# Turning the last third of one batch's tokens by DMA instead of on TensorE, under a new order of the whole program

## The chip, the cores and the metric

The kernel runs on one core of a Trainium2 chip. A core has several engines that run side by side, each with its own list of instructions: TensorE (PE: matmuls, with a weight load ahead of each), VectorE (DVE), ScalarE (ACT), GpSimd (POOL) and SyncE (SP, which here only issues DMAs). They wait for each other through semaphores. The metric is the device time of one execution in microseconds (us); the time of a kernel is the median of several executions.

## The reference

Sliding-window attention with four sink tokens for 4 batches, 8 heads, 768 tokens and 64 columns a head, and then a feed-forward layer on its output:

```python
keep = (pos[None, :] < 4) | ((rel >= 0) & (rel < 128))      # rel = query - key
scores = np.where(keep, q @ k.T / 8, -1e9)
a = softmax(scores)                                          # per row
x = (a @ v), heads side by side                              # 3072 tokens x 512
g = np.maximum(x @ w_in, 0) ** 2                             # w_in  512 x 2048
out = g @ w_out                                              # w_out 2048 x 512
```

Inputs and outputs are fp32; the kernel computes in bf16 with fp32 sums.

## The kernel before, in words

A batch b has 768 tokens: six tiles of 128 tokens (0 to 5), or three pairs of tiles s = 0, 1, 2. Its eight heads are four pairs m = 0 to 3. The work of a batch has these stages:

- **Loads.** For batch 1, q and k come with a cast to bf16 as `qn` (tokens on partitions), by DMAs that GpSimd issues (`load_cast`, L355); v likewise. Batches 2 and 3 do the same in `load_natural` (L383).
- **Turning q and k.** Scores need q and k with the head's columns on partitions (`qkT`). For batches 0 and 1 TensorE turns blocks of 128 x 128 by a matmul with the identity into PSUM (`pt`, L500), and VectorE or ScalarE copies PSUM to `qkT` (L191, L189). For batches 2 and 3 (the list `NATURAL`), SyncE issues one transposing DMA for each tile of q and of k (L454), straight from `qn` to `qkT`.
- **Scores** (L607), **exp** (ScalarE, L628), **mask** (two triangles on GpSimd, L215, or one product on VectorE, L640), **sink scores** and **sink_values** (the parts of the four sinks), **values** (L676, `po`), and **norm**: VectorE's reciprocal (L692) and product into `xn_sb` (L693).
- **Turning the attention output** (`xn_sb` to `xT`). For batches 0 and 1 two "bridge" operations for a pair of tiles turn it on TensorE (L725, into `px`), and two copies take it to `xT`. For batches 2 and 3 `turn_x` (L707) does it by a transposing DMA for each tile.
- **Layer 1** (`x @ w_in`; L757 for batches 0 and 1, seven products of a Strassen kind, L887, with sums on VectorE, L928 and L955, for batches 2 and 3), relu on ScalarE or VectorE (L768, L770), the square (L909, L911), and **layer 2** (L976, L1086), copies out of PSUM (`taken`, L1105) and the stores.

Batch 1's work is done in two groups of tokens: g = 0 is tiles 0 to 3, g = 1 is tiles 4 and 5 (the last third, s = 2).

The order is written out by hand or by a search, not found while the program runs. The kernel's functions only register operations with a `Plan`; `ORDER`, a text of operation numbers (a letter behind a number gives the engine where there is a choice), says in which order they are issued, and that is each engine's own program order. An operation that waits holds up everything behind it on its engine; so a DMA on SyncE that waits for its data holds up the DMAs behind it. Semaphore waits come from the data's dependencies, and from the reuse of buffers: PSUM pools att and den (two each), and SBUF pools (expm 8, r 3, sg 4, osb 2 and others).

`touch` (L196) keeps the list of instructions that use parts of one PSUM tile, and declares two of them independent when they are on different banks and either one of them is TensorE's, or both are marked `alone` and sit on different engines. `use` (L1067) calls it for layer 2's PSUM tile, `taken` copies one of its quarters out.

`NATURAL, TURNED, BIASED, FAST = (2, 3), (), 1, (2, 3)` (L1183) is the switch: `TURNED` lists the pairs of tiles of batch 1 whose attention output is turned by DMA, and it is empty. `BIASED` and `FAST` name where a mask is added by a matmul and where the seven products are used.

## Time and profile before

| what | value |
|---|---|
| median of 3 executions | 212.43 us (212.35 to 212.47) |
| the profiled execution's own time | 212.79 us |
| its span, from the first to the last instruction | 211.1 us |
| mean granted TensorE clock | 0.998 |
| busy TensorE, VectorE, ScalarE, GpSimd | 202.7, 171.3, 124.0, 98.0 us |

The profile is one execution. A line of a timeline or of the chain gives start, length, engine, line of the kernel, operation, output <- inputs and count. A line of the waits gives who waited for whom: us in total, times, longest. A line for a tile gives the groups of instructions that touch it with their shortest, median and longest duration in ns, and for DMAs the time from issue to landing.

A part of the page with the costliest groups that the steps below touch (busy us, mean ns of one, idle before and releaser):

```profile
L628 ACT ACTIVATE expm<-ps 128x1024 bf16<-128x1024 f32 (+1 forms) x48 | 43.7, 952 | 9.3 <-PE ps L607 9.1
L215 POOL TENSOR_SCALAR_AFFINE_SELECT expm<-expm 128x512 bf16<-128x512 bf16 x38 | 25.7, 707 | 43.5 <-ACT expm L628 39.2
...
L693 DVE TENSOR_TENSOR xn_sb<-po,rc 128x512 bf16<-128x512 f32 (+1 forms) x28 | 17.2, 615 | 1.0
...
L955 DVE CUSTOM_DVE_ANT_1 r<-pm,t 128x1024 bf16<-128x1024 f32 x12 | 14.6, 1221 | 0.8 <-PE pm L887 0.5
```

### The profile page before, as it was taken

What the parts mean: (1) busy time and instruction counts of PE and PEld (TensorE: products, weight loads), DVE (VectorE), ACT (ScalarE), POOL (GpSimd) and SP (SyncE); (2) the same over time, 40 slices, a digit from 0 to 9 for tenths busy, and PEclk for the clock granted to TensorE, in tenths of its full rate; (3) what the DMA queues carried; (4) which work ended last, traced back from release to release, by engine and by line L of the source; (5) the groups of instructions that cost most, each with busy time, mean ns of one, the idle gap of its engine ahead of it and who ended that gap; (6) DMA issues with size and microseconds to landing.
All of it is one profiled execution on the core that took longest, in us unless ns stands there. A gap on an engine that the chain in (4) does not pass through costs nothing.

```text
span 211.1 us, 5703 instructions
## 1 busy us (share of the span) xinstructions
PE 202.7 (96%) x2379; PEld 169.7 (80%) x2383; DVE 171.3 (81%) x321; ACT 124.0 (59%) x160; POOL 98.0 (46%) x139
## 2 busy tenths in 40 slices
PE   3999999999999999999999999899999999999993
PEld 3958997579568655579878988799799999999892
DVE  6487718569996766999897989999999869999863
ACT  2397187536774348868665158898772055797200
POOL 7798873599949952239205129950360000000000
PEclk9999999999999999999999999999999999999999
DMA  5999999999998999599999349395605322000214
GB/s 181 254 185 206 174 198 213 163 156 122 147 138 170 166 197 127 118 103 105 124 148 153 79 149 78 25 98 84 170 3 134 69 102 99 5 0 0 102 50 149
DMA packets 93881, 26.09 MB, mean 124 GB/s; under 512 B 86816, under 2 KB 91552, under 8 KB 93856
## 3 DMA queue, kind: packets, MB, share of 16 engines
q0 software_dynamic: 69248, 12.59, 81.1%
q1 hardware_dynamic: 24424, 13.07, 27.8%
q8 instruction: 18, 0.29, 0.6%
q10 hardware_dynamic: 184, 0.07, 0.1%
q14 instruction: 7, 0.06, 0.1%
HBM read 27.30 MB, written 6.29 MB: 159 GB/s over the span
## 4 chain that ended last, share of the span: by engine, by line
PE 89%; POOL 4%; DVE 3%; issue 1%; ACT 1%; POOLq 0%; DVEq 0%
PE py L1086 26%; PE pm L757 20%; PE pm L887 16%; PE py L976 7%; PE po L676 6%; PE ps L607 5%; PE pt L500 3%; POOL expm L215 3%; PE pt L182 2%; PE px L725 1%; DVE r L955 1%; PE ya L1086 1%; PE pk L566 1%; PE ps L600 1%; ACT expm L628 0%
## 5 line engine op out<-in xcount | busy, mean ns | idle before, releaser
L628 ACT ACTIVATE expm<-ps 128x1024 bf16<-128x1024 f32 (+1 forms) x48 | 43.7, 952 | 9.3 <-PE ps L607 9.1
L215 POOL TENSOR_SCALAR_AFFINE_SELECT expm<-expm 128x512 bf16<-128x512 bf16 x38 | 25.7, 707 | 43.5 <-ACT expm L628 39.2
L757 PE MATMUL pm<-xT,w_in_sb 128*128 128x256 bf16 (+1 forms) x320 | 44.7, 294 | 0.0
L757 PEld LDWEIGHTS <-w_in_sb 128*128 128x128 bf16 x320 | 34.2, 114 | 6.4 <-issue 0.8
L1086 PEld LDWEIGHTS <-gT_sb 128*128 128x128 bf16 x336 | 30.9, 98 | 3.8 <-issue 0.5
L1086 PEld LDWEIGHTS <-sg 128*128 128x128 bf16 x240 | 22.8, 98 | 3.3 <-issue 0.7
L768 ACT ACTIVATE r<-pm 128x1024 bf16<-128x1024 f32 x15 | 15.4, 1025 | 12.9 <-PE pm L757 12.0
L887 PEld LDWEIGHTS <-w_in_sb 128*128 128x128 bf16 x256 | 21.7, 114 | 0.7 <-issue 0.6
L1086 PE MATMUL py<-wt,gT_sb 128*128 128x256 bf16 x160 | 20.8, 273 | 0.0
L1086 PE MATMUL py<-wt,sg 128*128 128x256 bf16 x160 | 20.6, 273 | 0.0
L887 PE MATMUL pm<-xs,wi 128*128 128x128 bf16 (+1 forms) x192 | 19.5, 246 | 0.4 <-DVE r L955 0.3
L1086 PE MATMUL py<-w_out_sb,gT_sb 128*128 128x256 bf16 x144 | 18.7, 273 | 0.0
L909 ACT ACTIVATE gT_sb<-r 128x1024 bf16<-128x1024 bf16 x18 | 18.4, 1054 | 0.3
L693 DVE TENSOR_TENSOR xn_sb<-po,rc 128x512 bf16<-128x512 f32 (+1 forms) x28 | 17.2, 615 | 1.0
L676 PEld LDWEIGHTS <-expm 128*128 128x128 bf16 x352 | 16.4, 97 | 1.9 <-issue 0.5
L676 PE MATMUL po<-v,expm 128*128 128x65 bf16 x352 | 17.6, 193 | 0.2
L887 PEld LDWEIGHTS <-wi 128*128 128x128 bf16 x192 | 16.3, 114 | 1.7 <-issue 0.9
L928 DVE TENSOR_TENSOR t<-t,pm 128x512 f32<-128x512 f32 x24 | 16.0, 683 | 1.2 <-PE pm L887 0.6
L770 DVE TENSOR_SCALAR r<-pm 128x1024 bf16<-128x1024 f32 x9 | 11.0, 1222 | 7.1 <-PE pt L500 4.7
L189 ACT ACTIVATE osb<-py 128x256 f32<-128x256 f32 (+1 forms) x14 | 5.8, 413 | 17.6 <-DVE osb L1134 10.7
L976 PE MATMUL py<-w_out_sb,gT_sb 128*128 128x512 bf16 x60 | 15.1, 380 | 0.2
L955 DVE CUSTOM_DVE_ANT_1 r<-pm,t 128x1024 bf16<-128x1024 f32 x12 | 14.6, 1221 | 0.8 <-PE pm L887 0.5
(97 smaller groups left out, 379.1 us busy)
## 6 DMA issues: line engine op xcount, KB each, us to landing
out_dram<-osb SPq DMA_DIRECT2D x11, 512.0 KB, 2.9
v<-in_v_dram POOLq DMA_DIRECT2D x24, 128.0 KB, 6.1
qn<-in_k_dram POOLq DMA_DIRECT2D x20, 128.0 KB, 5.3
qn<-in_q_dram POOLq DMA_DIRECT2D x20, 128.0 KB, 5.8
w_in_sb<-in_moe_w_in_dram POOLq DMA_DIRECT2D x4, 512.0 KB, 9.4
w_out_sb<-in_moe_w_out_dram POOLq DMA_DIRECT2D x4, 512.0 KB, 11.1
qr<-in_k_dram SPq DMA_DIRECT2D x4, 256.0 KB, 5.2
qr<-in_q_dram SPq DMA_DIRECT2D x4, 256.0 KB, 4.8
```

What stands on the lines that cost most here:

```text
L215: nc.gpsimd.affine_select(out=e_tile, in_=e_tile, compare_op=ALU.is_ge, fill=fill, base=i - 1, pattern=[[0, n], [1 if i else -1, 128]], ch ...
L628: nc.scalar.activation(out=x[:, :, o:512], in_=bank_t["s", b, s, m][:, :, o:512], func=AF.Exp, scale=scale)
L676: touch(("po", b, s, m0), e, nc.tensor.matmul(pv[:, i, h2, :], lhsT=lhsT, rhs=rhs, start=(n_ == 0), stop=(n_ == len(mms) - 1)), j)
L693: touch(("po", b, s, m0), e, nc.vector.tensor_tensor(out=xn_sb[:, 2 * s:2 * s + 2, 128 * (m0 + j0):128 * (m0 + j0 + nj)].rearrange("p i (j ...
L757: nc.tensor.matmul(pm[:, i, :], lhsT=w_in_sb[:, fb // 4, kb, fb % 4:512:4], rhs=xT[:, c0 // 256:(c0 + cw) // 256, kb, :], start=(kb == 0), ...
L768: nc.scalar.activation(out=o, in_=h, func=AF.Relu)
L887: touch(tag, e, nc.tensor.matmul(y[:, bk, i, :], lhsT=weights(name, f0 + i, a), rhs=rhs[:, a, :], start=fresh and i == 0 and a == 0, stop= ...
L909: nc.scalar.activation(out=d, in_=x, func=AF.Square)
L928: touch(tag, e, nc.vector.tensor_tensor(out=T["t"], in0=T["t"], in1=T["y"][:, bk], op=ALU.subtract), bk)
L955: touch(tag, e, nc.vector._custom_dve(TENSOR_ADD_SAT, out=r.rearrange("p b n c -> p b (n c)"), in0=T["y"].rearrange("p b n c -> p b (n c)" ...
L976: touch((b, u), e, nc.tensor.matmul(pm[:, i, :], lhsT=gT_sb[:, fb, 128 * t:128 * t + 128], rhs=w_out_sb[:, fb, :], start=(fb == 0), stop=( ...
L1086: ins = nc.tensor.matmul(y_, lhsT=x[:, i, :], rhs=r_, start=(first or tail and n == 2) and i == 0, stop=i == HB - 1, skip_group_check=not ...
```

## The change

For batch 1's tiles 4 and 5, q, k and the attention output are turned by transposing DMAs on SyncE. Taken away are two TensorE operations of eight turns each with their four copies, and two bridges with their two copies; added are four DMAs qn to qkT and two DMAs xn_sb to xT. `taken` now marks its copies `alone=True`. The whole of `ORDER` from about its 95th entry on is another one, with new numbers, and with some operations on another engine.

```diff
-ORDER = """ ... """
+ORDER = """ ...
+... 45 46 47 48 49 248 109+1 50 51 52 53 54 361 ... 250
+362 208g 391g 363 364 365 366 367 368 369 370 ... 379 249 295 251 ...
+... 235+1 254+0+0 ... 261+0+0 ... 266+1 259+0 327 267 260 268 386 384 383 328a 318 395 333 396 398 329a
+317d 352 319d 353 334d 402 405 335d 269 330 403 411 331a 321 412 414 390 389 284 314 387 388 322a ... 415g
+... 377 378 593 594 595 596 420g ... 461 612 617 618 611 616 ... 425 ... 613 441 643 426 ... 442 ...
+"""
...
             copies = []
-            if b in NATURAL:
-                for s in range(NS):
+            if b in NATURAL or b == 1 and g:
+                for s in range(t0 // 256, last // 256):
...
-                    ops["cast", b, s] = ops["v", b, 2 * s + 1]
+                    if b in NATURAL:
+                        ops["cast", b, s] = ops["v", b, 2 * s + 1]
             w = 2 if n == 2 and t0 else 1
-            for m in range(0, NP, w) if b not in NATURAL else ():
+            for m in range(0, NP, w) if not b or b == 1 and not g else ():
...
-                            [c for m in ms for gg in range(g + 1) for c in ops["copies", b, m, gg]] +
+                            [c for m in ms for gg in range(g + 1) for c in ops.get(("copies", b, m, gg), copies)] +
...
-        def use(name, e, ins, c=None):
+        def use(name, e, ins, c=None, alone=False):
...
-                touch((b, u), e, ins, HOME[name][0])
+                touch((b, u), e, ins, HOME[name][0], alone=alone)
...
-                use(of, e, copy(e, t_[name], region(of)))
+                use(of, e, copy(e, t_[name], region(of)), alone=True)
...
-    NATURAL, TURNED, BIASED, FAST = (2, 3), (), 1, (2, 3)
+    NATURAL, TURNED, BIASED, FAST = (2, 3), (2,), 1, (2, 3)
```

Numbers of the new order that the text speaks of: 248 to 251 are the four new turns of q and k, 254 and 261 the scores of batch 1's s = 2, 266 and 259 its values, 267 and 260 their norms, 268 and 269 the two new turns of the attention output (tiles 4 and 5); 379 to 390 are turns of q and k of batch 2 (386 and 384 for tile 3, 383 for tile 2), 411 its first scores of s = 1 and 415 a mask of these; 391 and 208 are sink_values, 50 to 54, 361 to 378 and 593 on are loads; 461 is a store, 425, 426, 441 and 442 turn batch 2's attention output, 611 to 618 are turns of batch 3.

More of the change, by code (lines that the diff above doesn't have):

```diff
@@ L23 @@
 68d 69+1 85 70 71d 103+0 84+0 105 73g 74d 72d 23 75+1 86 76 77d 91+0 78a 24 87+1 93 25 89 88 92+0 80 26 114+1 90 94
-95+0 4 96 117 97 106g 99+1 98 104+0 107 100d 101 118g 81+1 102d 113+0 108d 156 115 127 82 116d 27 28 29 30 31 32 33
-34 35 36 37 38 39 40 41 42 43 44 109+1 119+0 121 111 157a 162 110 122 120 112 123+1 125 124d 126d 163a 164d 168 169d
-159 160a 161a 171 177 172a 158a 131 128 174 133a 129a 132a 178d 130d 144 137 165 146 140 170d 173d 175d 136 145 166a
-141d 167d 148 149d 289 290 138 139d 147d 134 291 292 135 179a 293 142 143 150 151 294 152 153a 295 154 155a 296 297a
@@ L28 @@
-298d 274 186 187d 188d 275 180 196+0 181a 182a 198d 183 197 199a 204+1 200+0 201 205 192+0 193 184d 185d 207d 194a
-203a 206a 195d 202d 209 276 189 190a 191d 300 208d 45 46 47 48 49 395g 50 51 52 53 54 365 366 367 368 369 370 371
-278 219+0+0 210+1 279 280 220 211 222 212+0+0 301 281 282 213 215 237+0+0 304 305 307 240 238 176a 241g 239g 302 214
-221 303 277 306d 216 310 223 230+0+0 233 231 234g 309a 372 232g 373 374 375 376 377 378 379 380 381 382 308 311
-224+0 242+0 385 383 386 299 384 312 315 225 235+0 283 243 313 314 316 236 317a 217+1 284 244+0 251+0 246 218 245d
@@ L33 @@
-286a 226+1 228 227a 229a 285 252d 247d 253d 399 287d 248+1 318 288 393 387 388 394 391 392 389 390 340 249d 250a 400
-254+0 255 402 331 256+0+0 259 257 341d 355 342d 332d 334 335a 258d 322 260g 263+0+0 323a 261+1 266 264 319 265g 358
-336d 262 267d 396 406 337 409 407 333a 320d 338a 268+0 328 270+0 401 321d 403 269 272 404 357 329a 359 273d 339d 325
-408 330d 405 271a 326a 324a 349 350a 327d 356 447 415 346 597 598 599 600 601 602 603 604 605 606 418 416 410 411
-352 448 360 466 419d 449 417d 412 347a 353a 354a 343 451 452 454 422 344d 453d 345a 450 348d 457 351d 467 485 486
@@ L38 @@
-455 423 458 456a 459 489 425 438 615 413 618 414 616 441 490 462 397 439 491a 398 492 431 460 424d 487 362 461 364
-463 488 464a 426d 363 494d 468 619 617 465 620 622 621 434 432 470 471 472a 420 427 421 428 495 435g 433g 442g 504a
-508 473 493 474 440d 475d 469 496 476 498 443 429 444 436 497 500 437 505 499 477 647 501 502d 430 445 446 503 523+0
-478 481 628 479 506 480 361 507 482 525a 650 648 651g 524 527 483a 631 509+0 526 528 634 632 529 530 510 511d 654
-513 531a 635 538 537 512 514 533 534 535 633 539 536d 657 655 515 516 638 517a 607 608 609 649g 658g 627g 610 656g
@@ L43 @@
-611 612 613 614 569+0 641 519 520 518a 642 636 521 571a 570 573 639 572 583+0 584 585a 640 574 637 522a 532a 575 587
-576 555+1 643 586 588 577a 557a 540 556 589 590 591a 578a 592a 579 580 679 558 581 559 561 593 594 560 595 541+0 562
-543a 542 545 680 544 546 644 683 563a 564a 596a 565 684 566 547 548 686 567 681 549a 626 624 623 625 645 484 646 670
-682 685a 551 552 687 673 671 674g 672g 688d 568d 689 553 629 690 630 554a 663 691 694 666 664 550d 692 582d 693 698
-699 675 676 717 665g 667g 695 702 652 653 659 703 705 668 704a 736a 696a 660 737 718 669 700 739 719 721 741+1 755+1
@@ L48 @@
-697 661 677 678 662 742 757a 707a 743a 701 708 738 723d 744 756 758 706 709 745 746 722 759 724 760 711 712 710 720
-740 761 747 713 714 727 748 715a 749a 762 725 772 726d 728 751 752 729 732 730 769 731 753 763a 750a 764a 733 734d
-770 815+0 765 766 817a 816 819 767 771 716 735 818 773+1 774 801+0 802 775a 754a 820 803d 776 768a 821 787+1 789a
-788 805 822 777 791 823a 804 806 807 825 826 808 778 829 790 830 792 824a 809a 810d 779 793 780 827 831 811 812 794
-781a 782a 828a 783 784 833 834 836 835a 795a 796a 797 798 832 785 813 839 799 838a 814a 837 840 841 844 786d 842
@@ L53 @@
-800a 848 849 843 852 853 855 854a 845 867 850 846a 871 868 872 857a 858 851 856 859 860 863 874 847 873d 861 869 862
-870 864 865d 866 877 876a 875 878 880 879 882 881 883 886 884 885
+95+0 4 96 117 97 106g 99+1 98 104+0 107 100d 101 118g 81+1 102d 113+0 108d 156 115 127 27 82 116d 28 29 30 31 32 33
+34 35 36 37 38 39 40 41 42 43 44 45 46 47 48 49 248 109+1 50 51 52 53 54 361 119+1 111 121 157a 158a 110 112 122 120
+162 123+1 125 168 163a 169a 126d 124d 171 172a 173d 165 166d 167a 159 131 128 130a 133a 132a 177 129d 160d 144 136
@@ new lines @@
+174 146 138 161d 178d 285 145 137 286 287 148 140 147d 139d 149d 164d 170d 141d 134 288 135 175a 150 142 289 290 143
+179d 151 152 291 154 176a 153a 292 270 293d 294d 271 155a 189 190a 200+0 272 202d 183 192+0 193 201 180 195a 203a
+194a 184d 196+0 204+0 205 197 198d 199d 191a 181a 207d 206d 185d 182d 186 209 212+0+0 215 213 187d 188d 296 297 250
+362 208g 391g 363 364 365 366 367 368 369 370 274 275 219+0+1 210+0 276 277 220 222 211 379 249 295 251 380 382 385
+381 237+0+0 240 238 300 301 302a 303 273 298 221 214 223 299 230+0+0 305a 306 216 239d 304 307 308 233 231 309 310
@@ new lines @@
+224+0 217+0 218 278 311 225 241g 371 372 242+0 226+0 228 234d 312 232g 313a 229a 243 227d 279 235+1 254+0+0 280 236
+244+1 246 351 392 245d 257 255 258g 373 374 375 256g 376 281 282a 261+0+0 264 247d 355 283d 324 252+0 315 262 354
+263d 265d 356 253 325a 336 316a 337a 338a 326a 266+1 259+0 327 267 260 268 386 384 383 328a 318 395 333 396 398 329a
+317d 352 319d 353 334d 402 405 335d 269 330 403 411 331a 321 412 414 390 389 284 314 387 388 322a 332d 397 406 399
+404 320a 339 415g 418 323d 340d 345 421 419 346a 422d 407 413d 462 463 408 443 348 349a 341a 400 401 464 342 444 360
@@ new lines @@
+445 377 378 593 594 595 596 420g 597 598 599 600 601 466 434 343a 350a 435 437 344a 467 447 448 409 614 410 615 347a
+465 449d 450 453 446 427 428 430 468a 451 454 452d 455 359 456 481 457 623g 429g 602 393 394 436g 438g 458 416 469
+459 460d 417 357 423 439 470 500a 482 503 424 502 472 483 431d 461 612 617 618 611 616 358 484 425 485 487a 486 471d
+504 440 488 432 473 475 490a 491 433 489 492 493 496 613 441 643 426 646 644 647g 494 624 495 476 501 497 498d 474
+477 499 519+0 521a 442 627 520 523 478 479d 522 524 628 630 505+0 507a 506 525 526 509 527a 650 631 508 510 651 511
@@ new lines @@
+512 513a 529 530 535 629 533 528d 653 531 603 604 605 606 607 608 609 645g 515 516 514a 634 654g 517 635 565+0 566
+534 610 579+0 567a 636 632 569 568 570 652g 581a 637 580 571 583 572 551+1 633 638 518a 620 622 619 621 573a 582 584
+639 552 553a 585 532a 536 555 586 554 587a 588a 640 575 576 557 556 577 675 578d 589 590 558 625 559a 537+0 538 539a
+561 626 540 560a 591 592a 574a 480 641 642 562 541 543 648 542 679 676 544 563 649 545a 732a 680 682 681d 677 685
+678 666 547 548 683 549 667 684a 669 564a 546a 668g 655 686 687 670d 656 659 550d 713 714 735 662 690 715 688 663d
@@ new lines @@
+733 736 716 717 718 671 719a 660 661g 672 737+1 720 723 689 721 664 724 665 694 739a 722a 738 741 751+1 725 753a 657
+658 673 734 740 743 752 755 726 691 742 744 728 754 757 696 692a 693 674 745a 747 698 695 756 727 729 766 765 767
+768 699 758 759d 700a 730a 746a 701 811+0 748 702 813a 761 812 749 704 697 762 769+1 763 771a 703a 764a 750a 814 815
+816 705 783+1 706 709 785a 760d 707 708 825 710 827 711a 784 817 787 786 770 818 819a 820a 773 772 797+0 798 788 774
+731 712 799d 789 821 822 823 775 776 790 801 791d 777a 778a 824a 829 779 793 794 780 792a 826 800 802 803 804 795
@@ L55 @@
+830 832 828 781 805a 831a 835 807 808 806a 782a 834a 796a 809 810d 833 836 837 840 844 845 846 838 863 839 847 841
+864 848 850a 849 851 852 855 853a 854 856 859 857 865 866 858 842a 843 867 868 870 869a 873 860 861a 862 871 874 875
+872d 878 876 877 882 879 881 880
 """
```

## The prediction

> **What bounds the kernel now.** I read the page's busy shares first, then the waits of TensorE, then the chain.

> ```profile
> PE 202.7 (96%) x2379; PEld 169.7 (80%) x2383; DVE 171.3 (81%) x321; ACT 124.0 (59%) x160; POOL 98.0 (46%) x139
> ...
> PE 89%; POOL 4%; DVE 3%; issue 1%; ACT 1%; POOLq 0%; DVEq 0%
> ...
> PE pt L182 <- POOL ident L239: 3.5, 1, 3.5
> PE pm L887 <- DVE r L955: 0.3, 1, 0.3
> PE pm L887 <- ACT t L189: 0.3, 1, 0.3
> PE px L725 <- DVE xn_sb L693: 0.2, 1, 0.2
> ```

> TensorE (PE) is busy 96% of the span, it makes 89% of the chain that ended last, and after its first 3.5 us it waits 0.8 us in all. So a matmul taken off TensorE is worth its whole time, if nothing new makes TensorE wait. VectorE (DVE) at 81% is next; the other engines have room on average.

> What the removed operations cost TensorE is read from starts in its timeline (start, length, then the instructions; the next start is what counts, since ends overlap):

> ```profile
> 71.33 0.61 PE L500 MATMUL pt<-ident,qn 128*128 128x128 bf16 x8
> 71.78 0.83 PE L725 MATMUL px<-ident,xn_sb 128*128 128x128 bf16 x12
> ...
> 73.85 0.62 PE L500 MATMUL pt<-ident,qn 128*128 128x128 bf16 x8
> 74.30 0.38 PE L757 MATMUL pm<-xT,w_in_sb 128*128 128x512 bf16 x1
> ...
> 90.07 0.61 PE L725 MATMUL px<-ident,xn_sb 128*128 128x128 bf16 x8
> 90.52 0.53 PE L676 MATMUL po<-v,expm 128*128 128x65 bf16 x12
> ```

> Eight turns hold the engine 0.45 us each time: 71.33 to 71.78, 73.85 to 74.30, 90.07 to 90.52.

> What the DMA turns that are already there cost is in the answers for the tiles they write (SyncE's issue: min/median/max ns; then from issue to landing, us):

> ```profile
> L454 SPq DMA_TRANSPOSE qkT<-qn x24: 1190/1223/2239, 59.7 to 146.4; - x24
> DMA to landing us min/median/max: 2.4/3.1/5.9
> ...
> L707 SPq DMA_TRANSPOSE xT<-xn_sb x12: 1192/1257/2057, 100.7 to 164.7; - x12
> DMA to landing us min/median/max: 2.4/2.5/6.5
> ```

> The third place to read is the stage of the seven products, where the chain leaves TensorE for VectorE:

> ```profile
> 130.95 1.23 DVE r L955
> 132.18 0.47 DVE expm L637
> 132.65 0.54 DVE xs L845
> 133.19 0.81 DVE gT_sb L911
> ...
> 134.60 1.22 DVE r L955
> 135.82 0.04 issue
> 135.87 2.78 PE pm L887 x24
> ```

> **The change part by part.**

> *Taken off TensorE.* Two transposes of eight matmuls (L500) and two bridges of four (L725): 3 x 0.45 = 1.35 us. Laying TensorE's two lists end to end with the durations of the rows gives 202.28 and 200.94, so −1.34. Nothing else is added to that engine.

> *Taken off VectorE and ScalarE.* Four copies pt to qkT and two px to xT. Two transposes are copied by one engine each half (VectorE 0.42, ScalarE 0.60), so about 3 x 0.42 = 1.3 us and 3 x 0.60 = 1.8 us go. The new order also gives ScalarE three squares (L909, 1.05 each; VectorE loses 3 x 0.81), VectorE one relu (1.22) and two masks (2 x 0.71), and GpSimd one sink_values that VectorE had. Together VectorE has about 3.2 us less, ScalarE 1.4 more, GpSimd about as much as before. None bounds on average, so the sums count for nothing by themselves; the stage of products is told below.

> *Added on SyncE: six DMA turns,* each 1.3 us of its queue (issues at 83.29, 84.60, 85.90 in the trace). The four of q and k need batch 1's last loads, which are now issued earlier; laid out, they land by 62 to 65, and the scores that read them (op 254) come at about 70: margin 5. At their worst (5.9 instead of 3.1) still 2. Cost 0. Their target has its four pieces far apart, where those of batches 2 and 3 lie together. The nearest row is xT's: pieces apart too, and 2.4 at best, as the others. So no surcharge.

> *The two turns of the attention output* and what stands behind them on SyncE is the tightest place. Batch 1's last values (ops 266, 259) end near 81.0; the reciprocal and product (0.20 + 0.69, L692/L693) with the starts between end near 82.15. Then SyncE issues turn_x of tile 4, then 386, 384, 383 (batch 2, tiles 3 and 2), 1.31 apart, so 383 begins near 86.05. In before, the turns of q and k weren't behind anything of batch 1's attention: the last of the eight issued from 80.55 began at 89.84, its scores at 94.45. Now op 411, the scores that read 383, is reached after four layer-1 operations of 1.75, two scores of 0.45 and small gaps, 8.06 us after those values. Slack = 8.06 − 1.15 − 3.93 − landing = 2.98 − landing. At the best landing (2.44, where no load runs) +0.5; at the median 3.1, a stall of 0.12; at 5.9 it is 2.9, at 6.5, 3.5. The rows at 84.60 and 85.90, the same time of the span, landed in 2.44 and 2.45; those of 5 to 6.5 us were issued at 100.7 to 103.3 behind loads. GpSimd's next loads in the new order (377, 378, 593 on) stand behind a mask (415) of op 411's own scores, so none runs here. I take the median's 0.12, with 0 and 3.5 as ends. Queued behind on SyncE are turn_x of tile 5 (lands about 89.8, first read about 91.35: margin 1.5), which the same wait doesn't reach, and the next turns.

> [...]

> *GpSimd's order.* The loads of batch 1's tiles 4 and 5 now stand ahead of sink_values (2.7 us each, two of them back to back). Masks for the values at op 235 and 259: laid out, they end near 68.85 and 77.4 where TensorE comes at 69.85 and 80.25. Margin 1.0 or more; cost 0. Before, TensorE lost 0.23 us near 67 on a mask whose two halves (1.24 us) were late; that stall goes: −0.23. Bounds: −0.23 to +1.7 (2.7 less the margin).

> *Stage of products, 128 to 141.* Before, the rows there leave 1.34 us that no matmul explains, VectorE being 16.79 of 18.00 us busy from 122 to 140. Walked through in the new order (three squares fewer, two masks more) I get about 1.05. TensorE arrives there earlier, and what VectorE can't match it gives back. Bounds: −1.34 (all gone) to +1.3 (all gain given back). I take 0, nearest to the walk.

> *Later.* Turns of batch 3 behind the store 461 keep 0.9 us or more to their scores; a turn_x (442) lands 1 to 2 us ahead of its sums where before it had 7. Cost 0, at most 2. *alone=True* lets a copy and its pair on another bank run side by side: 0, since two engines that aren't the bound gain; at best 0.1. End: the last product to the end is 3.7 us in both.

> Sum: −1.34 + 0.12 − 0.23 + 0 = −1.45. The profiled execution took 212.79 (span 211.1 and 1.69 around it), 0.36 above the median 212.43; the sum made against it is 211.34, and 210.98 at the median. **Forecast 211.0.** Its own range is 210.2 to 211.9.

> **The rivals.** A measurement here tells about 0.2%, 0.42 us: no change is 212.0 to 212.85.

> *R1, the products' stall goes as well.* For it: VectorE has 3.2 us less in the whole. Against: its masks grow just there. Time 211.0 − 1.34 = 209.7.

> *R2, the other side: turns land late at op 411.* Landings of 5.1 to 6.5 us are in the trace, and one wait in front of 386, 384, 383 delays all three. For it: no other place has so little slack. Against: landings of 2.44 to 2.45 at that time. [...] It is slower once the stall exceeds 1.97 us, that is from a landing near 4.95; from 4.1 it is no change.

> *R3, the gain is given back in the products,* since VectorE's work between 122 and 140 doesn't shrink as TensorE's start does: 211.0 + 1.3 = 212.3, no change. For it: VectorE 93% busy there. Against: the walk's 1.05.

> *R4, GpSimd is late with a mask,* by 1.7: 212.7; by both sink_values, 4.4 us, 215. Against: margin 1.0 in the walk.

> **How the numbers follow.** Forecast 0.53 (faster). R1 0.12 (faster). R3 0.11 (0.07 same, 0.04 faster). R2 0.15 (0.12 slower, 0.03 same). R4 0.06 (0.02 same, 0.04 slower). Something unseen in the new order, which renumbers nearly everything, 0.03 slower. Faster 0.53 + 0.12 + 0.04 = 0.69; same 0.07 + 0.03 + 0.02 = 0.12; slower 0.12 + 0.04 + 0.03 = 0.19. The range runs from 209.6 (most of R1) to 213.0 (R3 and the small ends of R2 and R4); about 0.03 lies below and 0.13 above.

> **What would show it.** TensorE's busy time near 201.4 with 2355 matmuls; no L725 or L500 of batch 1 after 70 us; 28 and 14 DMA turns; no wait of L607 on a turn of more than 0.2 us at 87 to 91; mask waits near 67 gone; gaps between 128 and 141 of about 1.1 us. Wrong if TensorE waits for qkT near 89 (R2), for expm before 80 (R4), or if the gaps at L887 grow by about what was freed (R3).

## The result: 3.4 per cent slower, and the profile after

The changed kernel took 219.79 us (median of four, 219.56 to 224.96), the kernel before 212.45 us beside it (212.35 to 212.68): a ratio of 1.034, 95% interval 1.032 to 1.036. 211.0 had been forecast. A ratio here comes from executions near the fastest of each kernel, so it can differ a little from the ratio of two medians. The profiled execution took 219.64 us, its span is 217.9 us; 6.8 us more than the span before.

The page of the changed kernel: busy time, then TensorE's granted clock and the DMA engines' busy share in 40 slices. The last line is the granted clock of the kernel before.

```profile
PE 204.6 (94%) x2359; PEld 169.6 (78%) x2359; DVE 170.9 (78%) x311; ACT 126.6 (58%) x162; POOL 98.1 (45%) x139
...
PEclk9999999999999999999799699999999999999999
DMA  6999999999999994699899549994011250200115
...
PEclk9999999999999999999999999999999999999999
```

TensorE has fewer matmuls and is busy longer: the clock line shows why, with two dips that the kernel before does not have. Its waits (us in total, times, longest):

```profile
PE pt L182 <- POOL ident L239: 3.5, 1, 3.5
PE ps L608 <- DMA qkT<-qn: 2.4, 2, 1.4
PE po L677 <- POOL expm L215: 2.2, 3, 0.9
PE pm L888 <- DVE t L929: 0.5, 1, 0.5
```

Two new waits, 2.4 us for a DMA turn and 2.2 us for masks. The stretches of three us around them (length, busy and number on PE, PEld, DVE, ACT, POOL, then granted clock, DMA share, GB/s):

```profile
100.00:103.00 3.00, 0.84 (x8) 0.29 (x6) 2.82 (x5) 1.59 (x2) 0.00 (x0) 0.94 1.65 147
103.00:106.00 3.00, 2.76 (x19) 1.85 (x20) 0.00 (x0) 2.43 (x3) 2.20 (x3) 0.50 0.19 16
...
115.00:118.00 3.00, 1.21 (x29) 0.86 (x25) 2.27 (x4) 1.06 (x1) 2.99 (x5) 1.00 1.35 157
118.00:121.00 3.00, 2.51 (x25) 1.97 (x26) 2.97 (x8) 0.00 (x0) 0.64 (x1) 0.78 1.20 180
121.00:124.00 3.00, 3.00 (x20) 2.30 (x19) 2.40 (x6) 0.38 (x1) 0.00 (x0) 0.65 0.63 125
```

After each gap the clock falls to half for some 3 us (0.50 from 102.64 to 106.06 and from 119.71 to 123.12) and matmuls take longer: eight of L1087 1.89 us at 103.89, and 1.04 at 99.36. The sum closes. The gaps between matmuls (those over 0.15 us, after the first 5 us) add up to 5.79 us, before to 0.76, so +5.03. The lower clock costs TensorE's busy time in a stretch times the share of the clock that is missing there: 2.76 x 0.50 + 2.51 x 0.22 + 3.00 x 0.35, and 0.08 in the stretches beside them, +3.06. The matmuls removed are −1.34, the prediction's own figure. Together +6.75 of the 6.8.

Where the first gap comes from is in SyncE's timeline (start, length, instruction) and in the chain that ended last:

```profile
75.13 1.24 SPq L454 DMA_TRANSPOSE qkT<-qn  x1
81.81 1.19 SPq L708 DMA_TRANSPOSE xT<-xn_sb  x1
83.10 3.88 SPq L454 DMA_TRANSPOSE qkT<-qn  x3
87.03 1.26 SPq L708 DMA_TRANSPOSE xT<-xn_sb  x1
88.46 2.50 SPq L454 DMA_TRANSPOSE qkT<-qn  x2
91.05 1.85 SPq L1000 DMA_DIRECT2D out_dram<-osb  x1
92.95 0.42 SPq L1164 DMA_DIRECT2D out_dram<-osb  x1
93.47 4.73 SPq L454 DMA_TRANSPOSE qkT<-qn  x2
```

```profile
93.47 2.45 SPq L454
...
96.01 7.18 DMA qkT<-qn
103.19 0.05 issue
103.24 0.72 PE ps L608 x8
```

SyncE is free at 76.4 and waits until 81.81 for the norms that the new turn_x needs; from there its queue has no gap until 98. The last two turns in the first fence are 387 and 388 (k of batch 2's tiles 4 and 5). They are issued at 93.47 and 96.01 and land 8.0 and 7.2 us later; the scores 434 stand ready at 100.5.

The second gap is in GpSimd's timeline:

```profile
93.28 1.78 POOL L408 DMA_DIRECT2D v<-in_v_dram  x2
95.04 1.77 POOL L396 DMA_DIRECT2D qn<-in_k_dram  x2
103.80 1.76 POOL L396 DMA_DIRECT2D qn<-in_q_dram  x2 [6.99 <-issue]
...
111.08 2.29 POOL L549 TENSOR_TENSOR vs<-vs_in,head_rows 32x130 bf16<-32x130 f32 x4
...
115.56 3.08 POOL L215 TENSOR_SCALAR_AFFINE_SELECT expm<-expm 128x512 bf16<-128x512 bf16 x4
```

The load 595 stands still for 7 us, until 388 has landed (at 103.19) and its buffer is free. The profile names no releaser for this wait; in the next run it names a turn from `qn` for the same load. Behind it are seven more loads, two masks, sink_values and, last, the masks 436 and 438, which TensorE needs at 115.5 and gets at 118.6.

### The profile page after: what moved, and what is told of

Same layout as the page of the kernel before. It is cut to its first block, busy times and chain, and to the rows that moved or that the text cites. A ratio compares the mean times of both kernels' runs of the same rounds, so it can differ in the third digit from the quotient of the medians.

```text
span 217.9 us, 5665 instructions
## 1 busy us (share of the span) xinstructions
PE 204.6 (94%) x2359; PEld 169.6 (78%) x2359; DVE 170.9 (78%) x311; ACT 126.6 (58%) x162; POOL 98.1 (45%) x139
## 4 chain that ended last, share of the span: by engine, by line
PE 76%; DMA 6%; DVE 5%; POOL 5%; SPq 3%; ACT 2%; issue 1%; DVEq 0%
PE py L1087 26%; PE pm L758 16%; PE pm L888 13%; PE py L977 7%; PE po L677 5%; PE ps L608 5%; DMA qkT<-qn 3%; DMA qr<-in_q_dram 3%; POOL expm L215 2%; POOL qn L396 2%; DVE t L929 2%; SPq L346 2%; PE pt L501 1%; SPq L454 1%; DVE r L956 1%
## 5 line engine op out<-in xcount | busy, mean ns | idle before, releaser
L215 POOL TENSOR_SCALAR_AFFINE_SELECT expm<-expm 128x512 bf16<-128x512 bf16 x34 | 23.7, 731 | 50.2 <-ACT expm L629 50.1
L1087 PEld LDWEIGHTS <-gT_sb 128*128 128x128 bf16 x336 | 31.9, 100 | 5.0 <-issue 0.8
L1087 PEld LDWEIGHTS <-sg 128*128 128x128 bf16 x240 | 23.4, 101 | 3.5 <-issue 0.5
L1087 PE MATMUL py<-wt,gT_sb 128*128 128x256 bf16 x160 | 22.2, 285 | 0.0
L1087 PE MATMUL py<-wt,sg 128*128 128x256 bf16 x160 | 21.9, 284 | 0.0
L769 ACT ACTIVATE r<-pm 128x1024 bf16<-128x1024 f32 x16 | 16.4, 1025 | 8.6 <-PE pm L758 8.6
L677 PE MATMUL po<-v,expm 128*128 128x65 bf16 x352 | 18.4, 193 | 2.4 <-POOL expm L215 2.2
L910 ACT ACTIVATE gT_sb<-r 128x1024 bf16<-128x1024 bf16 x19 | 19.4, 1055 | 0.6 <-DVE r L956 0.5
L1087 PE MATMUL py<-w_out_sb,gT_sb 128*128 128x256 bf16 x144 | 18.7, 273 | 0.0
L189 ACT ACTIVATE osb<-py 128x256 f32<-128x256 f32 (+1 forms) x15 | 5.9, 399 | 21.1 <-PE py L1087 12.9
L608 PE MATMUL ps<-qkT 64*128 64x128 bf16 (+1 forms) x256 | 15.2, 241 | 2.4 <-DMA qkT<-qn 2.4
L608 PEld LDWEIGHTS <-qkT 64*128 64x128 bf16 x256 | 8.3, 95 | 9.8 <-issue 5.1
L977 PE MATMUL py<-w_out_sb,gT_sb 128*128 128x512 bf16 x64 | 15.8, 380 | 0.0
```

What stands on the lines that cost most here:

```text
L215: nc.gpsimd.affine_select(out=e_tile, in_=e_tile, compare_op=ALU.is_ge, fill=fill, base=i - 1, pattern=[[0, n], [1 if i else -1, 128]], ch ...
L608: nc.tensor.matmul(ps[:, h2, o:o + w], lhsT=qkT_sb[r, m, 1, c, :], rhs=qkT_sb[r, m, 0, qb:qb + w // 128, :], start=(i == 0 and not biased) ...
L677: touch(("po", b, s, m0), e, nc.tensor.matmul(pv[:, i, h2, :], lhsT=lhsT, rhs=rhs, start=(n_ == 0), stop=(n_ == len(mms) - 1)), j)
L769: nc.scalar.activation(out=o, in_=h, func=AF.Relu)
L910: nc.scalar.activation(out=d, in_=x, func=AF.Square)
L977: touch((b, u), e, nc.tensor.matmul(pm[:, i, :], lhsT=gT_sb[:, fb, 128 * t:128 * t + 128], rhs=w_out_sb[:, fb, :], start=(fb == 0), stop=( ...
```

## The experiments

Letters name the theories as they stood when each run was planned. In some of these kernels a line number is one lower than in the changed kernel, since `ORDER` is wrapped to one line less. The first one, A: everything follows from 387 and 388, which are late behind two stores.

**The two turns ahead of the stores.**

```diff
-... 412 414 390 389 284 314 387 388 322a ...
+... 412 414 390 389 387 388 284 314 322a ...
```

> The new kernel with one move on SyncE: the turns 387 and 388 (batch 2, k of tiles 4 and 5) stand ahead of the stores 284 and 314 instead of behind them. Theory A (both stalls come from these two turns landing late: the scores 434 wait for them at 100.5 us, and GpSimd's load 595 waits for 388 to free its buffer and holds up the masks behind it): both turns are issued near 91.0 and 92.3 and land by 97, TensorE has no wait over 0.3 us at 100 to 104 nor at 115 to 119, the granted clock stays at 1.0, and the time falls by 7.5 to 8.5 us to 211.3 to 212.3. Rival B (GpSimd's order itself is late: loads and sink_values stand ahead of the masks 429, 436, 438): the first stall goes (2.4 us and some 1.4 of clock), the second stays, about 216. Rival D (SyncE's six more turns crowd its queue, so what is moved ahead only moves the delay): 218 or more.

218.59 us (215.76 to 220.34), ratio 1.031 (1.025 to 1.037). The wait for the turns is gone: 387 and 388 are issued at 92.1 and 94.7 and land in 3.8 and 4.6 us. The profile is of the shortest execution. In it a wait for masks stays, and the load 595 still waits for 388, though less long:

```profile
PE po L676 <- POOL expm L214: 1.6, 3, 0.8
...
POOL qn L395 <- DMA qkT<-qn: 2.0, 1, 2.0
```

So A is right about the first gap. For the second gap this run does not part A from B (GpSimd's order is late by itself): 388 landed at 99.3, not by 97, and the 2.0 us that the load waited for it are more than the 1.6 us by which the masks were late. A also missed how much the executions would differ.

A sixth buffer for `qn`, with which the load would not wait for 388 at all, does not fit into SBUF: another pool needs 2 KB a partition where 0.9 are left. So that test of the second gap is missing. The run with the attention output back on TensorE, below, comes nearest to it.

**The gaps filled, to see what lowers the clock.**

```diff
 DUMMIES = {
-    ... 119: 2,
+    ... 119: 2, 434: 43, 439: 45,
 }
```

> The new kernel with 43 spare matmuls ahead of the scores 434 and 45 ahead of the values 439 (about 0.056 us each, 2.4 and 2.5 us), which fill TensorE's two gaps and change nothing else. If the lower granted clock after each gap (0.50 at 103 to 106, 0.78 and 0.65 at 118 to 124) comes from the gap, it stays at 1.0, eight matmuls of L1087 take 0.88 us again, and the time falls by 2 to 3 us, to 216.8 to 217.8. If the clock falls for another reason, the time is 219.5 or more and the windows still show a lower clock.

The stretches of the same times in this kernel:

```profile
103.00:106.00 3.00, 3.00 (x40) 2.51 (x38) 0.59 (x2) 2.22 (x3) 2.64 (x4) 1.00 0.48 31
...
118.00:121.00 3.00, 3.00 (x30) 2.67 (x29) 2.97 (x8) 0.38 (x1) 0.00 (x0) 1.00 1.23 257
121.00:124.00 3.00, 3.00 (x47) 2.78 (x45) 2.96 (x9) 0.38 (x1) 0.00 (x0) 1.00 0.46 90
```

The clock stays at 1.00, and the same group of layer-2 matmuls (L1087 from gT_sb and w_out_sb) begins at 120.33 instead of 123.33, though both kernels are level at 103.89. Of these 3.0 us some 2.7 are the clock, near the 3.06 of the sum; the rest is a second gap that is 0.3 us shorter. So these two dips came from the idle gaps. The whole took 223.42 us all the same (one execution), as a third place opened, which its waits and chain show:

```profile
PE pm L888 <- DVE r L956: 5.7, 1, 5.7
```

```profile
131.97 7.89 DMA xT<-xn_sb
```

The turn 442 (batch 2's attention output, tile 5) is issued at 131.97, beside seven of GpSimd's loads (129.4 to 135.5) and a store, and takes 7.9 us; VectorE's sums and the seven products wait.

**The attention output back on TensorE, in the new order.** `TURNED` is `()`; the two turn_x go, and behind operation 333 stand two bridges and their copies.

```diff
-... 260 268 386 384 383 328a 318 395 333 396 ... 269 ...
+... 260 386 384 383 328a 318 395 333 (bridge) (bridge) (copy)d (copy)a 396 ...
-    NATURAL, TURNED, BIASED, FAST = (2, 3), (2,), 1, (2, 3)
+    NATURAL, TURNED, BIASED, FAST = (2, 3), (), 1, (2, 3)
```

> The new order with one part of the change undone: the attention output of batch 1's last third is turned on TensorE again (two bridges of four matmuls behind layer 1's operation 333, two copies), q and k are still turned by DMA. Theory A with the turn of the attention output as its origin (it holds SyncE from 76.4 to 81.8 waiting for the norms, so that everything behind it is 5.4 us late): 387 and 388 are issued before 91, both stalls go, and with 0.45 us more on TensorE the time is 211.5 to 212.6. Rival E (the new order's stores and loads make the turns late whatever holds SyncE before): 219 to 220.5.

216.72 us (one execution), between what A and its rival E had said. 387 and 388 are issued at 87.5 and 89.7 and land in 4.1 and 2.5 us: the turn_x did hold SyncE, and without it the first gap is gone. GpSimd's loads no longer wait for 388, and this is what is left of the second gap:

```profile
PE po L676 <- POOL expm L214: 0.7, 1, 0.7
```

So by this run some 0.7 of the 2.2 us of the second gap come from GpSimd's order by itself, and the rest from the late 388. The third place costs instead (442 takes 5.6 us beside loads; 2.6 us of waiting for L955 and a clock of 0.5 after it). Theory A was dropped here. In its place F: DMA turns land late whenever GpSimd's loads are in flight beside them, and the new order has several such places.

**The loads moved away from 387 and 388, the stores left ahead of them.**

```diff
-... 360 445 377 378 593 594 595 596 420g 597 ...
+... 360 445 420g 377 378 593 594 595 596 597 ...
```

> The new kernel with only GpSimd's loads 377, 378 and 593 to 596 moved behind the mask 420, so that they are issued from about 97 us instead of 93.3; the turns 387 and 388 stay behind the stores 284 and 314. If the loads beside them make these turns land 7 to 8 us after their issue, 387 lands within 5.5 us (by 99) and 388 within 6.5, and the first stall falls from 2.4 us to under 1. If the two stores ahead of them do it, both still take 7 to 8 us and the stall stays above 2.

216.29 us (one execution). The two turns, and the first of the loads that were moved:

```profile
93.94 3.56 SPq L453 DMA_TRANSPOSE qkT<-qn  x2
...
98.17 1.78 POOL L407 DMA_DIRECT2D v<-in_v_dram  x2
```

387 now lands after 4.46 us instead of 8.02, 388 is in time, and TensorE has no wait at 100 to 104. The turns still stand behind both stores, so the loads made the gap. The stores are not free either: 4.46 us is 2 more than the 2.44 of a turn with no load or store beside it. The masks are still late (2.4 us).

**The order alone: all six turns undone.** Two transposes, two bridges and six copies are put back into the new order.

> The new order with all six turns undone: batch 1's last third is turned on TensorE again, as before (two transposes, two bridges, six copies), everything else in the new order. Theory F (the new order itself puts DMA turns, loads and stores where they hold up each other: batch 2's last turns next to stores and loads at 93 to 104, the masks behind loads and sink_values at 108 to 118, batch 2's last turn of the attention output beside seven loads at 126 to 132): without the six turns the first stall goes, the other two stay, 215.5 to 219. Rival D (the six turns on SyncE are the cause): 212 to 213.5, which is the time before with the 0.2 us mask stall gone or an order a little worse.

219.85 us, ratio 1.034 (1.029 to 1.040), above F's range. In its trace the turn 442 costs 2.6 us, and no mask is late, against what F had said. Of its waits 1.6 us came from where the bridges were put (a relu of VectorE behind their copy), so they were put elsewhere and it was run again:

> The new order with all six turns undone, as in the run of the order alone, but with the two bridges and their copies two operations earlier in the order, where VectorE has no relu waiting behind them (in that run the copy made a relu late and cost TensorE 1.6 us and a lower clock, which is the place chosen for it and not the order). Theory F: that wait goes, the waits behind the loads (masks near 110 to 116, the turn 442 beside loads at 128 to 136) stay, 215 to 218.5. Rival D (the order alone costs nothing, the six turns cost it all): 212 to 213.5.

Four executions from 217.82 to 223.09 us, median 220.54. The profiled one (217.82) still has 1.9 us of waits near 90, beside the bridges, so the price of the order alone stays uncertain by about that; but the masks (0.8 us at 117.4) and the turn 442 (5.0 us from issue to landing, 0.7 us of waiting at 138) are there without any of the six turns. The order alone is not free, and D (it costs nothing) is out.

**The turns of q and k alone, in the order of before.** The four stand at the head of SyncE's turns.

```diff
-... 242+0 385 383 386 299 384 ...
+... 242+0 248 250 249 251 383 381 384 297 382 ...
```

> One part of the change alone in the order of before: q and k of batch 1's last third are turned by four DMAs, which stand at the head of SyncE's turns (about 53 to 59 us); the attention output stays on TensorE. Theory F: TensorE loses two transposes (0.90 us) and gains no wait, 211.2 to 211.9, ratio 0.994 to 0.998. Rival D: the turns crowd SyncE or the DMA engines, 212.4 or more.

216.44 us (214.58 to 219.15), ratio 1.011 (1.006 to 1.017): F had said 211.2 to 211.9 without a new wait, and its rival D 212.4 or more. The profiled execution is one of the longer ones, 218.01 us. How DMAs landed between 52 and 60 us (size, median us to landing), in the kernel before:

```profile
v<-in_v_dram POOLq DMA_DIRECT2D x3, 128.0 KB, 5.5
qn<-in_k_dram POOLq DMA_DIRECT2D x3, 128.0 KB, 5.1
qn<-in_q_dram POOLq DMA_DIRECT2D x2, 128.0 KB, 5.4
```

and with the four turns:

```profile
v<-in_v_dram POOLq DMA_DIRECT2D x4, 128.0 KB, 9.2
qn<-in_k_dram POOLq DMA_DIRECT2D x3, 128.0 KB, 8.5
qn<-in_q_dram POOLq DMA_DIRECT2D x2, 128.0 KB, 9.6
qkT<-qn SPq DMA_TRANSPOSE x4, 8.3
```

The DMA engines were busy in 9 tenths or more of nearly every slice up to 80 us. The turns landed by 64.9, some 13 us ahead of their own readers; the loads behind them landed 3 to 4 us later than before. (In the trace of *alone=True* below, without these turns, the same loads took 5.9 to 6.4 us; measured by that it is about 3.) The loads' own turns came later with them, and batch 2's scores waited 4.5 us near 73. The same, further back in the queue:

> q and k of batch 1's last third turned by DMA in the order of before, as in the run with the four turns at the head of SyncE's turns, but with them behind batch 2's first turns (from about 65 us). Theory G (the DMA engines are full until about 84 us, so four more turns, about 1.2 us of all sixteen engines each, make whatever stands behind them some 5 us late, wherever they go before then): a wait of TensorE of 1 to 5 us appears at the scores that read these turns (78 and 82) or at batch 2's scores (94), 213.5 to 217. Rival I (it was only the place, ahead of batch 2's first turns): no new wait, 211.2 to 212.2.

218.26 us (217.80 to 218.81), ratio 1.027 (1.024 to 1.030), above G's range. The mechanism of G holds, and rival I (it was only the place) is out. The wait is at the sink scores of batch 1's last third, which read the last of the four turns (251, issued at 72.18, landed 7.5 us later):

```profile
PE pk L567 <- DMA qkT<-qn: 4.9, 1, 4.9
```

**The turns of the attention output alone, in the order of before.** `TURNED` is `(2,)`; the two turn_x stand behind the norms, ahead of the next turn.

> The other part of the change alone in the order of before: the attention output of batch 1's last third is turned by two DMAs behind batch 2's eight turns (issued from about 91.1, when the norms have ended at 89.8), q and k stay on TensorE. TensorE loses two bridges (0.45 us). Layer 1's operation that reads it stands at about 92.2. Theory F: with two of GpSimd's loads beside them (issued at 90.4 and 91.3) the turns land at 94 to 96.5, TensorE waits 2 to 4 us there and loses 0.5 to 1.5 us more to a lower granted clock, 214 to 217.5. Without loads beside them they would land at 93.5 and 94.9: a wait of 1.3 to 2.7 us, 213.2 to 215.

220.33 us (219.60 to 221.10), ratio 1.035 (1.030 to 1.039): the turns were issued at 91.12 and 92.40, as said, and the second landed at 97.32.

```profile
PE pm L757 <- DMA xT<-xn_sb: 5.5, 1, 5.5
```

With 5.5 us of waiting the range of 2 to 4 us was too small, and the clock was at 0.50 from 96 to 102. TensorE was free for the reader at 91.95, so even a landing in 2.44 us would have left a wait of 2.9: about half of the 5.5 is the place where these turns stand here, and the rest their late landing.

**`alone=True` alone.**

> The kernel before with one part of the change alone: the copies out of layer 2's PSUM tile are declared independent of each other (alone=True). All theories: no measurable change, ratio 0.998 to 1.002.

213.06 us against 212.96; ratio 0.9998 (0.997 to 1.003): no effect.

**Three attempts to move things apart in the new order.** With 387 and 388 ahead of the stores, 442 ahead of the store 499, and the masks 436, 438, 429 ahead of the load 602 and sink_values 623:

> The new kernel with two of its three tight places moved apart: 387 and 388 ahead of the stores 284 and 314 and the turn 442 ahead of the store 499 on SyncE; the masks 436, 438, 429 ahead of the load 602 and sink_values 623 on GpSimd. The loads 603 to 609 stay behind the mask 647. Theory F: no wait at 100 to 104 nor at 110 to 119; what is left is the third place, the turn 442 beside the loads 603 to 609 (landing 3 to 8 us), so 211.5 if it lands within 3.5 us and up to 216.5 if it takes 6 or more. Rival H (the order is slow in many small places and not in these): 217 or more with waits elsewhere.

Four executions: 212.76, 216.40, 217.71, 217.90 us. The profile is of the longest: the turn 442 took 5.1 us, and its wait is 1.9 us; a mask on VectorE cost 1.1, where F had no wait, and a turn of q and k 0.9. The shortest is level with the kernel before; it has no profile, so what went better in it is not shown. With the loads 603 to 609 ahead of the mask 647 as well:

> The new kernel with its three tight places moved apart and nothing else: on SyncE 387 and 388 ahead of the stores 284 and 314, and the turn 442 ahead of the store 499; on GpSimd the masks 436, 438, 429 ahead of the load 602 and sink_values 623, and the loads 603 to 609 ahead of the mask 647 (which holds GpSimd idle for 12 us) instead of behind it. Theory F: no wait of TensorE over 0.5 us after 5 us, granted clock 1.0, 210.5 to 212.5. If a fourth place opens, 213 to 217, and the profile names it.

219.97 us (217.85 to 220.71). The places at 100, 115 and 130 are quiet, and the fourth opened: batch 3's turn issued at 119.57, beside the loads that had been moved, took 6.6 us, and its scores waited 2.9. With that block of loads split:

> As the kernel with two repairs, and the block of seven loads split: 603 to 606 ahead of the mask 647 (about 111 to 116), 607 and 608 behind it, 609 behind the mask 645. Theory F: four loads beside batch 3's turns at 112 to 120 make them land in at most 5 us, two loads beside the turn 442 let it land in at most 4.5 us; no wait of TensorE over 1 us after 5 us, 210.8 to 213. If even four loads push batch 3's turns past their scores at about 121, a wait of 1 to 3 us shows there, 213 to 216.

215.02 us (214.68 to 215.65), ratio 1.012 (1.009 to 1.015), the best of the steady ones, though above the 213 that F allowed: its waits are small (1.6 us for two turns, 0.6, 0.5, 0.4) and the clock stays at 1.0. With all loads behind the turns they might disturb:

> The new kernel with its DMA turns and GpSimd's loads moved apart at every place found so far: 387 and 388 ahead of the stores, the loads 377, 378 and 593 to 596 behind the mask 420, the masks 436, 438, 429 ahead of 602 and sink_values 623, the turn 442 ahead of the store 499, and the loads 605 to 609 behind the masks 645 and 654, so that only two loads run beside 442. Theory F: 387 and 388 land within 4 us, 442 within 4.5 us, no wait of TensorE over 1 us after 5 us, clock 1.0, 210.8 to 213. If the loads only become late at another reader (batch 3's turns at 141 to 147 and its scores near 150), a wait shows there and the time is 213.5 to 217.

221.83 us (219.22 to 224.18), ratio 1.031 (1.026 to 1.035): the loads 605 to 609 were issued from 136.4, batch 3's last turn landed at 148.57, and its sink scores waited 3.5 us, as the second case had it, though its range ended at 217; values waited 2.9 us more near 112 to 120, for a mask and for norms on VectorE. None of these beats the kernel before.

## Why the prediction was wrong

**What held.** The kernel is bound by TensorE, and the removed matmuls were worth what the rows said: −1.34 closes the sum above. Operation 411, named as the tightest place, did not wait: 383 was issued at 85.77, 0.3 from the 86.05 laid out. The mask stall near 67 is gone, and the products wait 0.5 and 0.2 us where they had 0.3 and 0.3. From the last product to the end it is 3.7 us. *alone=True* costs and gains nothing.

**What failed: "Added on SyncE ... Cost 0."** The new turns themselves came out as laid out: the four of q and k landed by 64.2. What was priced at nothing is what they do to the turns and loads behind them, and two things are wrong in that. First, landings. The prediction took the median of 3.1 us, with 5.9 as a worst case that the new turns' own margin of 5 had to bear. The median mixes two conditions. The sixteen traces of this study show the landing of 326 of their 638 turns. Here they are sorted by how many of GpSimd's loads were in flight: issued by 1.2 us after the turn's issue began (the issue takes about as long) and not landed when it began.

| loads in flight | turns | shortest, median, longest us to landing |
|---|---|---|
| 0 | 155 | 2.4, 2.7, 4.9 |
| 1 or 2 | 66 | 2.4, 3.3 and 4.0, 8.0 |
| 3 or 4 | 57 | 2.6, 5.0 and 4.8, 7.5 |
| 5 | 25 | 4.6, 6.2, 7.8 |
| 6 | 10 | 5.5, 6.5, 8.9 |
| 7 | 13 | 6.2, 7.8, 8.4 |

SyncE's own stores go with late landings too: of the 155 turns with no load, the 135 with no store known to be in flight have a median of 2.5 us, the 19 beside one store 4.1. The trace of before alone had the pattern: its twelve turns with no load beside them have a median of 2.5 us, the three with four to six loads took 4.2, 5.9 and 6.5. The prediction used this distinction for op 411, and for no other place. In the changed kernel a turn with no load beside it took 2.44 us and 387, beside which four loads and two stores ran, 8.02; moving the loads alone brought it to 4.46.

Second, what a turn does to others. The prediction asked when the new turns land, not what they delay. Where the DMA engines were busy for nine tenths or more of nearly every slice of the page of before, until about 84 us, four turns delayed the loads behind them by some 3 to 4 us in the order of before. In the new order the loads issued from 60 to 66 us took 7.8 to 10.8 us with the six turns, and 6.6 to 7.8 in the two runs of the order alone.

**"Queued behind on SyncE are turn_x of tile 5 ... and the next turns."** The list was right and was not followed to its end. SyncE's wait of 5.4 us for the norms was seen; that it pushes 387 and 388 from before GpSimd's loads of 93.3 to 96.8 to beside them wasn't. The run with that turn_x undone shows it: 387 and 388 land by 92.2. "Stand behind a mask (415) of op 411's own scores, so none runs here" was true of op 411 and is exactly why the loads start when the scores have run, in front of 387.

**"GpSimd's order ... cost 0"** was walked up to 77.4 only. The masks of 113 to 118 stand behind loads and sink_values, and the first of those loads behind a buffer that 388 frees. The range of −0.23 to +1.7 was for other masks; the measured wait is 2.2, of which the order by itself leaves 0.7 with the attention output on TensorE, and 0.8 and nothing in the two runs of the order alone.

**"Later ... Cost 0, at most 2."** The margin of 1 to 2 us of turn 442 was read correctly and priced at the landing of a quiet time. In the changed kernel it held by luck, as the loads began 0.7 us after the turn's issue (132.36 against 131.64); in five of the runs above it cost 0.7 to 5.7 us.

**A term that no step had: the clock.** Every step priced a wait at its own length. Here 5.0 us of gaps cost 3.1 us more.

**The rivals.** R2 had the mechanism, at another operation: 2.4 us at op 434, where a stall of 2.9 to 3.5 had been worked out for op 411 from landings of 5.9 and 6.5. R2 needed the second gap and the clock beside it to reach 219.8; with 0.15 it was held too unlikely, because each place was looked at alone. With no load beside them turns landed in 2.4 us at best, and beside loads in up to 8.9.

What stays open: how the 6.8 us divide. Each part alone costs 1 to 3.5 per cent in the order of before, the order alone between 1.4 (the shortest execution of the second try, less its 1.9 us beside the bridges) and some 3.5, and together they cost 3.4, so they do not add. And why executions of one kernel differ by 5 us in the new order: that a landing decides each time whether a gap opens is argued, not shown. The clock alone does not explain it: three executions of the order alone took 219.55, 219.62 and 220.08 us at mean granted clocks of 0.984, 0.999 and 0.992.

## What to carry to other kernels

Work that went from a busy engine to DMA turns met other transfers here: a median landing of 2.7 us with no load in flight and of 7.8 with seven, and loads 3 to 4 us later behind four turns. Sort the landings of the profile by what else was in flight, and price both the landing beside the loads and the delay of the loads behind. Where an operation waits on a queue, follow the queue to its end and ask beside which transfers each of its later entries now runs. On a bound TensorE, price a gap at its length plus what the clock takes after it (here 5.0 us and 3.1).

## What the runs showed of the hardware that was not expected

Part of what decided may be when a wait falls. In the changed kernel's trace the clock is at 0.50 from 102.64 to 106.06, from 119.71 to 123.12 and, after the last matmul, from 218.70 on. The starts lie 17.07 and 98.99 us apart, 5 and 29 times the 3.413 us that each of the two dips inside the kernel lasts. Cut into stretches of that length from these starts, this trace has TensorE busy for 47% and 56% of the stretch just ahead of the two dips (99.23 to 102.64, 116.30 to 119.71), and for 77% or more of every other whole one from 3.65 us to the last matmul. That such stretches say why the other waits above left the clock at 1.00 is not shown, and it is not the whole rule: in the profile of the four turns at the head, whose dip starts at 77.88, TensorE was busy for 48% of the 3.41 us from 71.06, and the clock stayed at 1.00 up to 76.

What a dip cost was steady here. After waits of 1.6 to 4.9 us the clock was at half speed for 3.41 us in the changed kernel, and for 3.40 to 3.44 us by the windows of eight other kernels, which is up to 1.7 us lost. After the waits of 5.5 and 5.7 us it was 6.84 us by the windows, from about 95.7 to 102.5 in the first, part of it while TensorE still waited.
